# Attention and two feed-forward blocks on one core: splits spread over a border, norms and masks reordered, a small addition moved to GpSimd

## The chip, the cores and the metric

The kernel runs on 1 core of one Trainium2 chip. The metric is the device time of one execution in microseconds. In the profile PE is TensorE (matmul and transpose), PEld its weight loads, DVE VectorE, ACT ScalarE, POOL GpSimd, and SP the engine whose queue issues nearly all transfers. Every engine works through its own instructions strictly in their order and waits for the others by semaphores.

## The reference

```python
q_assign = argmax(q_n . c_n); k_assign = argmax(k_n . c_n)      # per head, 16 clusters
mask     = q_assign[:, :, :, None] == k_assign[:, :, None, :]
scores   = where(mask, scale * q @ k.T, -1e9)
attn     = exp(scores - max); attn = attn / (sum(attn) + 1e-9)
x        = (attn @ v), heads side by side                       # 1536 x 512
x        = ((x @ w1) * (x @ w2)) @ w3 @ w_out                   # 512 -> 1024 -> 1024 -> 512
h        = x @ w_in
out      = (max(h, 0) + alpha * min(h, 0)) @ moe2_w_out         # 512 -> 2048 -> 512
```

There are 2 batches, 8 heads, 768 positions and 64 numbers per head, all in float32.

## The kernel before

**Attention.** A head is a unit of 6 tiles of 128 queries, so there are 96 tiles; the loop at the end of the listing walks over them with index i. In step i the engines get, in this order: the transposes of tile i-4 (`emit_T`, L502), the scores of tile i+1 (`emit_S`, L462 for the products and L463 for the part that carries the cluster masks), for every second tile the sums' reciprocal (`emit_r`), the multiplication by it of tile i-2 (`emit_norm`, POOL, L488), the copies of the transposed tile out of PSUM (`emit_evac`, half on ACT L509, half on DVE L510), the row maximum of tile i+1 (`emit_max`, DVE, L470) and the exponential of tile i (`emit_exp`, ACT, L477); every second step ends with the products with v (`emit_PV`, L519). The scores have two PSUM buffers, the transposed tile one pair.

**Heads.** While a unit runs, the next head is prepared by `h_split` in pieces 0 to 5: piece 0 is three operations on POOL (L421, L422, L426), pieces 1 to 3 are copies by DMA, piece 4 sends the two cluster masks (L440, L441), piece 5 loads the head after it. A table by tile of the unit says which piece goes out when.

**Jobs.** `job(b, g)` works out the masks of four heads; its steps, and later the steps of the first layers, are spread over the attention steps by a generator (`fill`). The norms' square root stands in it (ACT L325) and needs another table on ACT than the exponential.

**Weights.** Each float32 weight tile is split into a high part and a low part (products are made of three fp32r matmuls). `w_step` does it in two halves: `w_conv` on DVE (L183, L184, L187; "a conversion" below), then the cast of the high part on ACT and the subtraction for the low part on POOL (L232). `w_goal` does one half, `w_pairs` loads tiles that were split before and kept in DRAM.

**The border.** The first layers of batch 0 (`l1`, tiles l1a and l1b, 12 matmuls each) run as fill work; l1a goes out through ACT, l1b through DVE (L580) which writes the product into PR. After them `x_split` splits the attention output of batch 1 (ACT L556; low parts on DVE and POOL, L558) into the buffer that batch 0's matmuls have just read, `p_split` splits the products PR of batch 0 (ACT L785, DVE L786: tile pl), and the first layers of batch 1 follow, with blocks of w3 (`lc`) between them. PR of batch 1 takes the same memory as PR of batch 0: as a new tile it can only be written when all splits of batch 0 are done. The PSUM tiles of this part are a ring of five, so TensorE may be at most five tiles ahead of what DVE and ACT have emptied.

Of the kernel before, what the change touches and what calls it, by code (L numbers as in the profile page):

```python
# [12 lines left out]
ALU = mybir.AluOpType  # L13
# [15 lines left out]
def kernel(  # L29
# [14 lines left out]
    nc = tc.nc  # L44
# [26 lines left out]
    seq, at, keep, need = [], {}, {}, {}  # L71
# [47 lines left out]
    NSEQ = len(seq)  # L119
# [116 lines left out]
    def w_goal(n):  # L236

        w_pairs(n)
        w_step(n)
# [213 lines left out]
    def emit_S(i):  # L453
        if i >= NU:
            return
        u, qt = unit(i)
        s = ST[u]
        t = pst("s", [P, 2, 512], f"s{i}", bufs=2)
        q = slice(qt * P, qt * P + P)
        for a in range(2):  # L460
            ks = slice(a * HS, a * HS + HS)
            nc.tensor.matmul(t[:, a, 0:HS], lhsT=s[:, 0, q], rhs=s[:, 1, ks], start=True, stop=False)  # L462
            nc.tensor.matmul(t[:, a, 0:HS], lhsT=s[0:80, 2, q], rhs=s[0:80, 3, ks], start=False, stop=True)  # L463
        scp[i] = t
# [16 lines left out]
        pt[i] = p  # L481

    def emit_r(g):
        nc.vector.tensor_scalar(out=sums[g], in0=sums[g], scalar1=1e-9, scalar2=None, op0=ALU.add)
        nc.vector.reciprocal(out=sums[g], in_=sums[g])  # L485

    def emit_norm(i):
# [61 lines left out]
    XS, PR = {}, {}  # L549
# [18 lines left out]

    def l1(b, f, a, alloc):

        if b not in PR:
            PR[b] = cp.tile([P, 8 * S], F32, tag="pr", name=f"pr{b}").rearrange("p (f s) -> p f s", f=8)
        t = alloc(f"l1a{b}{f}{a}")
        l1_mm(t[:, 0:HS], b, f, 0, a)
        q = wp.tile([P, HS], F32, tag="asb", name=f"asb{b}{f}{a}")
        nc.scalar.copy(out=q, in_=t[:, 0:HS])
        yield
        t = alloc(f"l1b{b}{f}{a}")
        l1_mm(t[:, 0:HS], b, f, 1, a)
        nc.vector.tensor_tensor(out=PR[b][:, f, a * HS : a * HS + HS], in0=t[:, 0:HS], in1=q, op=ALU.mult)  # L580
        yield


    with tc.manual_schedule():
# [46 lines left out]
        def l1_steps(b, f, ahead):  # L631
            for a in range(2):
                if a == 0:
                    w_ready(("l1", b, f, 1))
                for _ in l1(b, f, a, alloc_f):
                    w_goal(ahead)
                    yield f
# [10 lines left out]
        def fill_steps():  # L648

            yield from j01  # L650
            jm = cp.tile([P, 8 * S], F32, tag="wox", name="jm1")
            PR[0] = cp.tile([P, 8 * S], F32, tag="pr", name="pr0").rearrange("p (f s) -> p f s", f=8)
            sn = PR[0][:, 5:7].rearrange("p f s -> p (f s)")
            jmem[1, 0] = jm, jm[:, 3072 : 4608], jm[:, 5376 : 6144]
            jmem[1, 1] = jm, sn, PR[0][:, 7]
            for c in range(3):
                j_load(1, 0, c)
                yield
            j10, j11 = job(1, 0, alloc_f), job(1, 1, alloc_f)
            for k in range(5):  # L660
                next(j10)
                yield
            j_load(1, 1, 0)
            next(j10)
            yield
            for k in range(6):
                if k < 2:
                    j_load(1, 1, k + 1)
                next(j11)
                yield  # L670
            for _ in j10:
                yield
            for _ in j11:
                yield
            for _ in range(4):
                w_goal(at["l1", 0, 0, 1])
                yield
            while len(xdone) < 4:
                yield
            for f in range(8):  # L680
                yield from l1_steps(0, f, at["l1", 0, f, 0] + 3 if f < 6 else at["l1", 1, 0, 1])


        cur = [alloc_s]
# [10 lines left out]
            next(j00)  # L695
        next(j01)
        emit_S(0)
        emit_max(0)
        for _ in j00:
            pass  # L700
        cur[0] = alloc_r
        for k in range(2):
            next(j01)
        cur[0] = alloc_f
        nc.scalar.activation(out=warm, in_=warm, func=AF.Exp)
        nc.gpsimd.tensor_scalar(out=alp, in0=alp, scalar1=-1.0, scalar2=1.0, op0=ALU.mult, op1=ALU.mult)
# [7 lines left out]
        for i in range(NU + 8):  # L714
            if 0 <= i - LT < NU:
                emit_T(i - LT)
            if i + 1 < NU:
                emit_S(i + 1)

            if i >= 7 and i % 2 == 1 and (i - 7) // 2 < NU // 2:  # L720
                emit_x((i - 7) // 2)
            if i >= 2 and i % 2 == 0 and i // 2 - 1 < NU // 2:
                emit_r(i // 2 - 1)
            if 0 <= i - 2 < NU:
                emit_norm(i - 2)
            if 0 <= i - LT < NU:
                emit_evac(i - LT)
            if i + 1 < NU:
                emit_max(i + 1)
            if i < NU:  # L730
                emit_exp(i)
                u, j = unit(i)
                for k in ((0,), (1, 2), (3,), (4,), (5,), ())[j]:
                    h_split(u + 1, k)
            if i >= NU or i % 2 == 1 or i < 24 or 40 < i < 56:
                if fill_at[0] < (L1_B if i < NU else L1_D):
                    if next(fill) is not None:
                        fill_at[0] += 1
            if 10 <= i < 30 and i % 2 == 0:
                w_goal(at["l1", 0, 2, 0])  # L740
            if NUH + 4 <= i < NUH + 8:
                x_split(0, i - NUH - 4, 0)
                x_split(0, i - NUH - 4, 1)
                xdone.append(i)
            if i == NU - 1:
                late.append(i)
                for k in range(2):
                    w = st_tile(f"wo{k}").rearrange("p a n -> p (a n)").rearrange("p (g t n) -> p g t n", g=3, t=2)
                    for g in range(3):
                        WO[3 * k + g] = w[:, g, 0], w[:, g, 1]  # L750
            if i >= NU - 1:
                w_goal(at["wo", 0, 3, 0])

            k = i - 6
            if k >= 0 and k % 2 == 0 and k // 2 < NU // 2:
                emit_PV(k // 2)
                if k % 12 == 10:
                    v_load(k // 12 + 2)
# [31 lines left out]
        WO[6], WO[7] = (w[:, 0, 0], w[:, 0, 1]), (w[:, 1, 0], w[:, 1, 1])  # L790
        WO["wc"] = xp.tile([P, 2, 8, 512], F32R, tag="wc", name="wc")
        nsp = 0
        for f in fill:
            if f is not None and f < 7:
                w_goal(at["wo", 0, 5, 0])
            if f is not None and nsp < min(f, 6):
                p_split(0, nsp, 0), p_split(0, nsp, 1)
                nsp += 1
        for a in range(2):
            for p in range(4):  # L800
                x_split(1, p, a)
        while nsp < 8:
            p_split(0, nsp, 0), p_split(0, nsp, 1)
            nsp += 1
        for n, f in enumerate(BLOCKS):
            if f >= 0:
                for _ in l1_steps(1, f, NSEQ):
                    pass
            else:
                w_ready(("w3", 0, ~f, 1))  # L810
                lc(~f, alloc_c, lambda k: w_goal(NSEQ))
# [128 lines left out]
```

## Time and profile before

| what | us |
|---|---|
| median of 3 runs | 797.45 (797.44 to 798.0) |
| the profiled execution | 797.35 |
| its span, first to last instruction | 795.4 |
| TensorE busy in it | 758.0 |
| TensorE idle in it | 37.4 |

The kernel is bound by TensorE, so a time is read from the places at which TensorE is idle and from those at which its granted clock is halved. The attention lies from 22 to 314 us, the border from 314 to 370 us, and what follows is outside the change.

### The profile page before, as it was taken

To read this page: it belongs to the slowest core of one execution; us is meant where nothing else is said; L and a number is where in the kernel's file an instruction comes from. 1 tells how busy PE (TensorE), PEld (TensorE's weight loads), DVE (VectorE), ACT (ScalarE), POOL (GpSimd) and SP (SyncE) were. 2 spreads that over 40 slices of the span, in tenths; PEclk is the share of its full clock that TensorE was granted. 3 is DMA by queue.
4 is the path that set the end of the run, shared out by engine and by line. 5 is a ranking of instruction groups with operands and counts; after the bars stand their busy time and mean duration, and the time that the engine had idled before them with its cause. 6 is when DMAs were issued, how large, how long until landed. Compare 5 with 4: busy or idle time off the path is not lost.

```text
span 795.4 us, 13428 instructions
## 1 busy us (share of the span) xinstructions
PE 758.0 (95%) x5073; PEld 685.5 (86%) x5073; DVE 496.0 (62%) x833; ACT 393.5 (49%) x836; POOL 250.7 (32%) x228
## 2 busy tenths in 40 slices
PE   5789889989999999879999999999999999999998
PEld 2677778879999989879988999999998888899996
DVE  3778798995767777798455689324547763223222
ACT  5678766674555664364233345235444444333232
POOL 0466565684555633253222333001112220000000
PEclk9899999999999999989999999999999999999999
DMA  8657454253545517736444498016566637433332
GB/s 249 182 177 246 124 156 119 67 121 80 143 114 153 173 51 245 269 129 202 157 161 157 156 314 295 15 43 208 174 212 190 208 122 275 132 133 126 118 128 79
DMA packets 38863, 127.31 MB, mean 160 GB/s; under 512 B 5168, under 2 KB 5296, under 8 KB 38800
## 3 DMA queue, kind: packets, MB, share of 16 engines
q1 hardware_dynamic: 38800, 126.46, 50.8%
q8 instruction: 40, 0.66, 0.3%
q14 instruction: 23, 0.19, 0.1%
HBM read 84.08 MB, written 28.31 MB: 141 GB/s over the span
## 4 chain that ended last, share of the span: by engine, by line
PE 81%; DVE 5%; POOL 3%; issue 3%; ACT 3%; DMA 2%; SPq 1%; POOLq 0%; ACTq 0%; DVEq 0%
PE l L249 8%; PE l L251 8%; PE l L250 8%; PE t L502 7%; PE o L519 7%; PE acc L251 5%; PE acc L250 5%; PE acc L249 5%; PE s L463 4%; PE s L462 4%; PE l1a L250 3%; PE l1a L251 3%; PE l1a L249 3%; PE l1b L249 2%; PE l1b L251 2%
## 5 line engine op out<-in xcount | busy, mean ns | idle before, releaser
L232 POOL TENSOR_TENSOR wh<-wt,wh 128x512 fp32r<-128x512 f32 x64 | 86.7, 1355 | 241.3 <-ACT wh L231 120.7
L488 POOL TENSOR_SCALAR p<-p,su 128x768 f32<-128x768 f32 x96 | 88.6, 931 | 105.8 <-DVE su L485 44.1
L854 DVE SCALAR_TENSOR_TENSOR gr<-gr,alp 128x384 f32<-128x384 f32 x64 | 41.7, 651 | 109.1 <-ACT gr L853 109.1
L470 DVE TENSOR_REDUCE nm<-s 128x1 f32<-128x768 f32 x96 | 91.5, 953 | 10.4 <-PE s L463 8.6
L502 PE MATMUL t<-cst,p 128*128 128x128 f32 x576 | 85.0, 283 | 7.0 <-DVE pt L510 3.9
L477 ACT ACTIVATE p<-s,nm 128x768 f32<-128x768 f32 x96 | 87.0, 907 | 7.4 <-DVE nm L470 5.7
L502 PEld LDWEIGHTS t<-cst,p 128*128 128x128 f32 x576 | 66.5, 144 | 19.3 <-issue 7.3
L462 PE MATMUL s<-st 128*128 128x384 f32 x192 | 74.9, 390 | 3.6 <-ACT p L477 3.6
L251 PE MATMUL acc<-wh,g 128*128 128x512 f32 x192 | 75.3, 392 | 0.0
L249 PE MATMUL acc<-wh,g 128*128 128x512 f32 x192 | 74.8, 390 | 0.6 <-ACT os L878 0.6
L250 PE MATMUL acc<-wh,g 128*128 128x512 f32 x192 | 75.3, 392 | 0.0
L184 DVE SCALAR_TENSOR_TENSOR wt<-wr,wt 128x512 uint32<-128x512 uint32 x72 | 73.0, 1014 | 2.5
L519 PE MATMUL o<-pt,vs 128*64 128x128 f32 x1152 | 74.4, 279 | 0.0
L519 PEld LDWEIGHTS o<-pt,vs 128*64 128x64 f32 x1152 | 62.6, 138 | 12.5 <-issue 12.3
L852 ACT ACTIVATE gr<-l 128x384 f32<-128x384 f32 x64 | 31.2, 488 | 83.6 <-PE l L251 83.6
L463 PE MATMUL s<-st 80*128 80x384 f32 x192 | 67.0, 349 | 2.8 <-DMA st<-mk 2.8
L857 ACT CAST g<-gr 128x384 fp32r<-128x384 f32 x64 | 32.8, 513 | 58.7 <-DVE gr L854 58.7
L509 ACT COPY pt<-t 128x384 f32<-128x384 f32 x96 | 45.9, 478 | 31.6 <-PE t L502 30.9
L510 DVE COPY pt<-t 128x384 f32<-128x384 f32 x96 | 52.7, 549 | 12.3 <-PE t L502 11.3
L187 DVE SCALAR_TENSOR_TENSOR wt<-wu,wt 128x512 uint32<-128x512 uint32 x72 | 58.1, 808 | 2.5
L858 DVE TENSOR_TENSOR g<-gr,g 128x384 fp32r<-128x384 f32 x64 | 35.7, 558 | 37.1 <-ACT g L857 37.1
L231 ACT CAST wh<-wt 128x512 fp32r<-128x512 f32 x64 | 39.7, 620 | 32.8 <-DVE wt L187 13.8
(132 smaller groups left out, 1796.2 us busy)
## 6 DMA issues: line engine op xcount, KB each, us to landing
wh<-kept SPq DMA_DIRECT2D x58, 512.0 KB, 3.5
wr<-in_w_dram SPq DMA_DIRECT2D x48, 512.0 KB, 5.0
kept<-wh SPq DMA_DIRECT2D x48, 512.0 KB, 5.6
wr<-in_w3t_dram SPq DMA_DIRECT2D x16, 512.0 KB, 4.2
jm<-in_qka_dram SPq DMA_DIRECT2D x12, 512.0 KB, 5.3
hr<-in_qkh_dram SPq DMA_DIRECT2D x16, 384.0 KB, 3.5
st<-st SPq DMA_DIRECT2D x16, 384.0 KB, 3.7
st<-st SPq DMA_DIRECT2D x32, 192.0 KB, 2.7
```

The source lines that it names most:

```text
L184: nc.vector.scalar_tensor_tensor(out=t, in0=r[:, :, 0], scalar=29, in1=t, op0=ALU.logical_shift_right, op1=ALU.bitwise_or)
L232: nc.gpsimd.tensor_tensor(out=lo, in0=tts.pop(n), in1=f32(hi), op=ALU.subtract)
L249: nc.tensor.matmul(o, lhsT=whi, rhs=xhi, start=first, stop=False)
L250: nc.tensor.matmul(o, lhsT=whi, rhs=xlo, start=False, stop=False)
L251: nc.tensor.matmul(o, lhsT=wlo, rhs=xhi, start=False, stop=last)
L462: nc.tensor.matmul(t[:, a, 0:HS], lhsT=s[:, 0, q], rhs=s[:, 1, ks], start=True, stop=False)
L463: nc.tensor.matmul(t[:, a, 0:HS], lhsT=s[0:80, 2, q], rhs=s[0:80, 3, ks], start=False, stop=True)
L470: nc.vector.tensor_reduce(out=m, in_=scp[i][:, :, 0:HS], op=ALU.max, axis=AX.XY, negate=True)
L477: nc.scalar.activation(out=p.rearrange("p (a k) -> p a k", a=2), in_=scp.pop(i)[:, :, 0:HS], func=AF.Exp, bias=nmax.pop(i), scale=1.0, acc ...
L488: nc.gpsimd.tensor_scalar(out=pt[i], in0=pt[i], scalar1=sums[i // 2][:, i % 2 : i % 2 + 1], scalar2=1.0, op0=ALU.mult, op1=ALU.mult)
L502: nc.tensor.transpose(t[:, k], pt[i][:, kt * P : kt * P + P], ident)
L519: nc.tensor.matmul(ob[g][64 * j : 64 * j + 64], lhsT=v[:, u % 2, kt], rhs=pth[g][:, kt, j * P : j * P + P], start=(kt == 0), stop=(kt == N ...
```

## The change

There are five edits.

1. `emit_r` adds 1e-9 on POOL instead of DVE; the reciprocal stays on DVE.
2. The steps of `job(0, 1)` that make the norms of the second four heads are issued ahead of the first row maximum and of the first masks' writes.
3. Piece 4 of `h_split` (the masks) goes out with piece 3, one tile of the unit earlier than before; the other pieces keep their places.
4. Between i = 10 and 50 the weights' half steps are taken every fourth tile, where they were taken every second tile from 10 to 30. Conversions on DVE now stand at i = 12, 20, 28, 36 and 44, and stood at 10, 14, 18, 22 and 26.
5. PR of batch 1 is the same tile as PR of batch 0, so that its eighths are written as soon as the eighth's own split is done. Ahead of `x_split` two of the eight splits are made instead of six, the other six are spread over the first layers of batch 1. Two conversions move across in the same direction.

```diff
 def emit_r(g):
-    nc.vector.tensor_scalar(out=sums[g], in0=sums[g], scalar1=1e-9, scalar2=None, op0=ALU.add)
+    nc.gpsimd.tensor_scalar(out=sums[g], in0=sums[g], scalar1=1e-9, scalar2=1.0, op0=ALU.add, op1=ALU.mult)
     nc.vector.reciprocal(out=sums[g], in_=sums[g])
...
 def l1(b, f, a, alloc):
+    if b == 1:
+        PR[1] = PR[0]
...
-                yield from l1_steps(0, f, at["l1", 0, f, 0] + 3 if f < 6 else at["l1", 1, 0, 1])
+                yield from l1_steps(0, f, at["l1", 0, f, 0] + 3 if f < 6 else at["wo", 0, 3, 0] if f < 7 else at["l1", 0, 7, 1])
...
         emit_S(0)
+        cur[0] = alloc_r
+        for k in range(2):
+            next(j01)
         emit_max(0)
         for _ in j00:
             pass
-        cur[0] = alloc_r
-        for k in range(2):
-            next(j01)
...
-                for k in ((0,), (1, 2), (3,), (4,), (5,), ())[j]:
+                for k in ((0,), (1, 2), (3, 4), (), (5,), ())[j]:
                     h_split(u + 1, k)
...
-            if 10 <= i < 30 and i % 2 == 0:
+            if 10 <= i < 50 and i % 4 == 0:
                 w_goal(at["l1", 0, 2, 0])
...
-        for f in fill:
-            if f is not None and f < 7:
-                w_goal(at["wo", 0, 5, 0])
-            if f is not None and nsp < min(f, 6):
+        def more(n):
+            nonlocal nsp
+            if nsp < n:
                 p_split(0, nsp, 0), p_split(0, nsp, 1)
                 nsp += 1
+        for k, f in enumerate(fill):
+            w_pairs(at["l1", 1, 1, 1])
+            if f is not None and f < 7 and k % 2 == 0:
+                more(3)
         for a in range(2):
             for p in range(4):
                 x_split(1, p, a)
-        while nsp < 8:
-            p_split(0, nsp, 0), p_split(0, nsp, 1)
-            nsp += 1
         for n, f in enumerate(BLOCKS):
             if f >= 0:
-                for _ in l1_steps(1, f, NSEQ):
-                    pass
+                for k, _ in enumerate(l1_steps(1, f, NSEQ)):
+                    if f < 3:
+                        w_goal(NSEQ)
+                    if k % 2 == 0:
+                        more(8)
```

TensorE's own order does not change anywhere. The rows below show the other engines' orders at three places; the number behind a name tells buffers apart.

On DVE, behind `x_split`, before (pl is a low part of a split of batch 0, wt three operations of a conversion, pr the product of a pair of tiles of batch 1):

```order
L786 TENSOR_TENSOR pl_4071<-pr_488,ph_4070 128x384
L786 TENSOR_TENSOR pl_4075<-pr_488,ph_4074 128x384
L183 TENSOR_SCALAR wt_4281<-wu_4158 128x512
L184 SCALAR_TENSOR_TENSOR wt_4281<-wr_4092,wt_4281 128x512
L187 SCALAR_TENSOR_TENSOR wt_4281<-wu_4158,wt_4281 128x512
L580 TENSOR_TENSOR pr_4257<-l1b_4287,asb_4271 128x384
L183 TENSOR_SCALAR wt_4322<-wu_4285 128x512
L184 SCALAR_TENSOR_TENSOR wt_4322<-wr_4124,wt_4322 128x512
L187 SCALAR_TENSOR_TENSOR wt_4322<-wu_4285,wt_4322 128x512
L580 TENSOR_TENSOR pr_4257<-l1b_4328,asb_4316 128x384
```

The same engine and place now:

```order
L582 TENSOR_TENSOR pr_490<-l1b_4248,asb_4230 128x384
L183 TENSOR_SCALAR wt_4264<-wu_4240 128x512
L184 SCALAR_TENSOR_TENSOR wt_4264<-wr_4057,wt_4264 128x512
L187 SCALAR_TENSOR_TENSOR wt_4264<-wu_4240,wt_4264 128x512
L183 TENSOR_SCALAR wt_4291<-wu_4268 128x512
L184 SCALAR_TENSOR_TENSOR wt_4291<-wr_4107,wt_4291 128x512
L187 SCALAR_TENSOR_TENSOR wt_4291<-wu_4268,wt_4291 128x512
L788 TENSOR_TENSOR pl_4069<-pr_490,ph_4068 128x384
L788 TENSOR_TENSOR pl_4073<-pr_490,ph_4072 128x384
L582 TENSOR_TENSOR pr_490<-l1b_4303,asb_4285 128x384
```

Between two pr there was one conversion; now there are two and a split, four times in a row (the six pairs of tiles get C S pr, four times C C S pr, then S pr, with C a conversion and S a split; before they got S S, then six times C pr).

On POOL, at the border between units 5 and 6, before (hr and st are the pieces of the next head, p the attention rows, su their sums):

```order
L421 TENSOR_SCALAR hr_1282<-hr_1282,cst 128x768
L422 TENSOR_SCALAR st_1350<-hr_1282 128x768
L426 TENSOR_TENSOR st_1350<-hr_1282,st_1350 128x768
L488 TENSOR_SCALAR p_1322<-p_1322,su_1279 128x768
L488 TENSOR_SCALAR p_1348<-p_1348,su_1347 128x768
```

The same engine and place now:

```order
L421 TENSOR_SCALAR hr_1249<-hr_1249,cst 128x768
L422 TENSOR_SCALAR st_1323<-hr_1249 128x768
L426 TENSOR_TENSOR st_1323<-hr_1249,st_1323 128x768
L488 TENSOR_SCALAR p_1295<-p_1295,su_1246 128x768
L484 TENSOR_SCALAR su_1320<-su_1320 128x2
L488 TENSOR_SCALAR p_1321<-p_1321,su_1320 128x768
```

The addition L484, for which DVE's reciprocal waits, now stands behind the head's three operations and one multiplication.

On SP, at the masks of unit 2, before (jm is the load of 512 KB for the masks of batch 1, hr a head, mk the masks):

```order
L436 DMA st_412<-st_412 64x768
L265 DMA jm_487<-in_qka_dram 128x1024
L440 DMA st_412<-mk_210 16x768
L441 DMA st_412<-mk_210 16x768
L265 DMA jm_487<-in_qka_dram 128x1024
```

The same queue and place now:

```order
L436 DMA st_412<-st_412 64x768
L440 DMA st_412<-mk_210 16x768
L441 DMA st_412<-mk_210 16x768
L265 DMA jm_489<-in_qka_dram 128x1024 x2
L401 DMA hr_552<-in_qkh_dram 128x768
```

The masks go out directly behind the head's last copy, and the first load of jm behind them.

## Rows read from the trace of the kernel before

**Rows 1.** The page: busy time, share and instructions of TensorE.

```profile
PE 758.0 (95%) x5073; PEld 685.5 (86%) x5073; DVE 496.0 (62%) x833; ACT 393.5 (49%) x836; POOL 250.7 (32%) x228
```

**Rows 2.** Waits of PE: who <- for whom: us in total, times, longest.

```profile
PE l1a L249 <- ACT xs L556: 5.7, 1, 5.7
...
PE t L502 <- DVE pt L510: 3.9, 4, 1.7
PE s L462 <- ACT p L477: 3.6, 2, 2.9
...
PE s L463 <- DMA st<-mk: 2.8, 2, 2.1
PE t L502 <- POOL p L488: 2.1, 4, 1.1
```

**Rows 3.** Windows: start:end us, busy us by engine, PEclk, DMA share, GB/s.

```profile
53.00:57.00 4.00, 4.00 (x25) 3.10 (x28) 2.47 (x5) 1.55 (x4) 1.79 (x2) 0.57 0.89 352
...
94.00:98.00 4.00, 4.00 (x34) 3.67 (x29) 2.05 (x5) 2.21 (x6) 3.59 (x4) 0.57 0.00 0
...
340.00:346.70 6.70, 3.69 (x10) 3.29 (x11) 6.63 (x13) 6.34 (x16) 3.18 (x2) 0.50 0.15 62
```

**Rows 4.** Timeline at unit 2's masks: start, duration, instruction, [idle before].

```profile
47.71 0.54 SPq L265 DMA_DIRECT2D jm<-in_qka_dram  x1
...
48.30 0.56 SPq L440 DMA_DIRECT2D st<-mk  x1
...
52.12 1.06 ACT L278 ACTIVATE jm<-jm 128x1024 f32<-128x1024 f32 x1 [0.56 <-DMA jm<-in_qka_dram]
```

**Rows 5.** Timeline, TensorE behind the conversion of i = 22.

```profile
92.50 0.55 PE L502 MATMUL t<-cst,p 128*128 128x128 f32 x3 [1.75 <-DVE pt L510]
```

**Rows 6.** Timeline at i = 36 to 38, where a conversion is put in.

```profile
126.46 0.95 DVE L470 TENSOR_REDUCE nm<-s 128x1 f32<-128x768 f32 x1
...
127.81 0.56 DVE L510 COPY pt<-t 128x384 f32<-128x384 f32 x1
...
128.50 0.82 PE L502 MATMUL t<-cst,p 128*128 128x128 f32 x6
```

**Rows 7.** Timeline at the border of units 5 and 6, DVE and POOL.

```profile
114.93 1.83 POOL L426 TENSOR_TENSOR st<-hr,st 128x768 fp32r<-128x768 f32 x1
116.74 1.78 POOL L488 TENSOR_SCALAR p<-p,su 128x768 f32<-128x768 f32 x2
...
115.02 1.77 DVE L484 TENSOR_SCALAR su<-su 128x2 f32<-128x2 f32 x1
```

**Rows 8.** Timeline, TensorE in the first layers of batch 1.

```profile
341.84 0.69 PE L249 MATMUL l1a<-xs,wh 128*128 128x384 f32 x1 [5.74 <-ACT xs L556]
...
343.70 0.69 PE L250 MATMUL l1a<-xs,wh 128*128 128x384 f32 x1 [1.17 <-DVE xs L558]
...
357.50 0.33 PE L249 MATMUL l1a<-xs,wh 128*128 128x384 f32 x1
...
359.58 0.33 PE L249 MATMUL l1b<-xs,wh 128*128 128x384 f32 x1
```

**Rows 9.** Timeline of DVE and POOL about the border of the batches.

```profile
328.74 1.80 DVE L786 TENSOR_TENSOR pl<-pr,ph 128x384 fp32r<-128x384 f32 x2 [1.10 <-ACT ph L785]
...
343.52 6.27 POOL L558 TENSOR_TENSOR xs<-xr,xs 128x384 fp32r<-128x384 f32 x4 [4.03 <-ACT xs L556]
...
355.21 0.55 DVE L580 TENSOR_TENSOR pr<-l1b,asb 128x384 f32<-128x384 f32 x1
...
358.51 0.55 DVE L580 TENSOR_TENSOR pr<-l1b,asb 128x384 f32<-128x384 f32 x1
```

**Rows 10.** Timeline of DVE: two conversions in a row, later on.

```profile
412.20 0.42 DVE L183 TENSOR_SCALAR wt<-wu 128x512 uint32<-128x512 uint32 x1
...
413.99 0.42 DVE L183 TENSOR_SCALAR wt<-wu 128x512 uint32<-128x512 uint32 x1
...
415.17 1.66 DVE L187 SCALAR_TENSOR_TENSOR wt<-wu,wt 128x512 uint32<-128x512 uint32 x1
```

## The prediction, on record before the changed kernel ran

> **What bounds the kernel now.** The first thing to read is the page's line of busy times [rows 1]: TensorE works 758.0 of 795.4 us, every other engine far less. A change that takes no product away can gain only in the 37.4 us in which TensorE idles and in the stretches in which its clock is halved. So I read the waits of TensorE next [rows 2]: 5.7 us for the first high part of x (xs), 2.8 us for masks (st<-mk), 2.1 us for the multiplication on POOL (p), 3.6 us for exponentials. The windows [rows 3] add what such a wait leaves behind: behind the mask wait (53 to 57 us) and the wait at i = 22 (94 to 98) the granted clock is 0.57 on the mean, and from 340.0 to 346.7 it is 0.50, the lower level of 1.2 GHz, behind 5.74 us without work. The timelines [rows 4 to 10] then tell what each wait hangs on. The profiled execution took 797.35 us against a median of 797.45, so the sum is made on 797.35 and the 0.1 us is left out.
>
> **The change, part by part.** TensorE's order stays, so each part is a question of what TensorE waits for.
>
> *A. Norms ahead of the first maximum and masks.* Nothing is added. The first attention tile waits for its exponential (3.6 us over two waits, [rows 2]); norms issued earlier put some small DVE and ACT work ahead of the first maximum, but the square root then has left ACT before the first masks, and the next masks come sooner. I take -0.5 us, between -1.0 (a third of that wait) and +0.5.
>
> *B. Masks a tile earlier.* On SP the masks of unit 2 are issued at 48.30 us, behind a jm load issued at 47.71 [rows 4], and TensorE waits 2.10 of the 2.8 us [rows 2] for them at 52.76. Now they go first, so they are ahead of 512 KB in the queues. Removed: 2.10, the 0.7 of unit 5, and in 53 to 57 us 0.43 of 4.00 us of clock, so 1.7 [rows 3]: 4.5 in all. Against it: the jm load is issued some 1.2 us later (two issues of about 0.56 and their gaps), and ACT's square, which at 52.12 had already waited 0.56 us for it [rows 4], comes later by as much; products of the next masks stand behind it on TensorE in the same stretch. So most of the first wait is changed for another and the clock may fall all the same. I take -2.0, between -4.5 and +0.6 (the jm delay alone, half of 1.2).
>
> *C. Conversions spread over i = 12 to 44.* Five conversions are moved, none added up to there. At their old places TensorE waited four times for the copy of pt that stood behind one on DVE, 3.9 us in all [rows 2], 1.75 of it at i = 22 [rows 5], and behind that one the clock lost 0.43 of 4 us, 1.7 [rows 3]. Of the 1.75 I leave 0.8 to ACT's change of tables, so -4.8. At the new places from i = 28 on the step is at its tightest: from the maximum at 126.46 to the transposes at 128.50 are 2.04 us, of which the maximum and the copy (0.95 and 0.56) leave 0.5 [rows 6]. A conversion takes 1.79 us (412.20 to 413.99, [rows 10]), so it puts the copy behind it, and TensorE, about 1.3 us back; that for i = 28, 36 and 44 is +3.9. Net -0.9, between -4.8 (slack in the two PSUM buffers hides them) and +0.6 (a price of 1.8 each).
>
> *D. The addition on POOL.* At the border of units 5 and 6 POOL's last operation for the next head runs from 114.93 to 116.76, and DVE's addition to two numbers, started at 115.02, takes 1.77 us and ends with it [rows 7]. So DVE is blocked there whichever way the addition goes. Now the addition stands on POOL behind that operation and behind one multiplication as well, two of which take 1.78 us [rows 7]. DVE's reciprocal waits for it, and behind the reciprocal on DVE are queued the copy of pt and the next maximum, for which TensorE and then ACT wait. It is held by one multiplication (0.89) and two hand-overs longer than before, by my estimate 1.12 us. By the order on POOL this happens at the units' borders from i = 12 to 30, five times; at one of them two multiplications are ahead (2.09). Total 4 x 1.12 + 2.09 = 6.6 us, of which I charge 0.6, +4.0, because the copy of the odd tile has some of the 0.5 us of rest. Against it a few blocked additions away from the borders are gone and part of the 2.1 us of waits for POOL [rows 2], -0.5. So +3.5, between -0.5 and +6.6. After some 180 us TensorE is never late by so much that this shows.
>
> By the Trainium skill, "SBUF — State Buffer", section "Who interferes with whom", DVE and POOL share a port pair, and whoever issues first holds it for the whole instruction while the other is fully blocked; the trace agrees with the 1.77 us that end with POOL's operation. By the rule taken alone an addition off DVE frees DVE, and D would be -0.5 or better. The order on POOL speaks against that, so my sum doesn't use it.
>
> *E. The border.* This is the largest. Removed: TensorE stops 5.74 us for the first xs and 1.17 for its low part, and runs the tile between at half the clock [rows 8, 3], where it loses half of the 4.9 us that it works from 341.84 to 346.7, 2.45. Now four splits of batch 0 fewer lie ahead of `x_split`, so the casts of xs can follow the last matmul at 336.10 (341.84 - 5.74). That is up to -9.4 us at the first tile of batch 1.
>
> But the splits come back on DVE, between products. A tile of 12 matmuls takes 2.08 us (357.50 to 359.58, [rows 8]), a pair 4.16, and before one pair cost DVE 3.30 us (355.21 to 358.51, one conversion and pr, [rows 9]): DVE kept up. Now four pairs in a row need two conversions, a split and pr. A conversion alone takes 1.79 us and one directly behind another 2.84 (413.99 to 416.83, [rows 10]), since POOL's subtraction for the first blocks it; a split's low parts end 2.90 us after the conversion (1.10 waiting for ACT's ph, then 1.80, [rows 9]); pr 0.55, overlapping by some 0.1. That is about 7.9 us a pair against 4.16. TensorE may be five tiles ahead, no more, so it is held back by 3.7 us for each pair once the ring is full. The chain: TensorE could begin at about 336.7; POOL's four xs subtractions take 6.27 us [rows 9], to 343.1, and slow the conversions of the first pair; its split and pr end at 346.8. The first w3 block needs the tile of the fourth pair: 346.8 + 3 x 7.9 = 370.5. Before, it began at 341.84 + 1.17 + 2.45 + 12 x 2.08 = 370.4. So the 9.4 us are given back in whole; and the block's second half (2.8 us later before) now needs a conversion that stands behind the splits, about 1.0 to 1.5 us late. I take +1.5, between -7 (DVE keeps pace, the POOL subtractions still cost 2) and +4 (a halved clock through the waits).
>
> Sum: -0.5 - 2.0 - 0.9 + 3.5 + 1.5 = **+1.6 us**, so 797.35 + 1.6 = 799.0, with the 0.1 us to the median 799.1.
>
> **The rivals.**
>
> *R1, DVE keeps pace at the border (faster).* The cycle of 7.9 us is built from contended durations. Bare, it is 2 x 1.79 + 1.0 + 0.5 = 5.0. TensorE's own work would then end at 336.7 + 12 x 2.08 = 361.7, and the chain gives 346.8 + 3 x 5.0 = 361.8, 8.6 us before 370.4; the late conversion of the block costs 1.5 of it, so E is about -7 and the time 799.1 - 1.5 - 7 = 790.6. It decides from a cycle of 7.4 us down (1.5 / 3 less than 7.9), from which on E is a gain. For it: the blocked part varies in the rows. Against it: each conversion is followed by its POOL subtraction.
>
> *R2, the holds and late conversions are hidden (faster).* If the tiles' double buffers take the 1.1 us of D and the 1.3 of C, D is -0.5 and C -4.8: 799.1 - 4.0 - 3.9 = 791.2. For it: TensorE idles only 2.1 us for POOL now. Against it: a single conversion stopped TensorE for 1.75 us [rows 5].
>
> *R3, holds and conversions cost in full (slower).* One mechanism: an in-order DVE is stopped behind a POOL operation or a conversion, and TensorE by the whole of it: D +6.6, C +0.6, E +4: 799.1 + 3.1 + 1.5 + 2.5 = 806. It decides as soon as D and E together exceed by 1.6 us the 3.4 that A, B and C bring.
>
> *R4, the change does not do what it says.* The masks wait for the producer anyway, and xs waits for ACT's queue, not for the splits: B and E about 0, C and D together +2.6 or less: 797.5 to 800.
>
> **How the numbers follow.** Forecast 0.37 (797 to 802), R1 0.20 (790.6), R2 0.15 (791), R3 0.14 (806), R4 0.14. A difference of 0.2%, 1.6 us, is about what a measurement of this kernel can tell from none: 795.85 to 799.05. Faster: R1, R2 and 0.01 of the forecast, 0.36. Same: 0.17 of the forecast and half of R4, 0.24. Slower: 0.19, R3 and the other half, 0.40. The predicted time is 799.1; the range takes in R1 and R2 and the lower part of R3, 790.5 to 805.5; the likeliest case's own is 797 to 802.
>
> **What would show it.** A: the first exponential wait of TensorE under 2.9 us. B: no wait for st<-mk near 52 us; if instead one for ja of about 1 us stands there with the clock at half, the exchange is right. C: none of the four old waits for pt, and three waits for pt of about 1.3 behind i = 28, 36 and 44. D: reciprocals with an idle of 1 us or so before them, put down to POOL's su, at five borders. E: the first l1a of batch 1 by 337 with waits under 1 us, then TensorE waiting for pr about 3.7 us a pair from the third pair on, and w3's first block beginning near 370.5. It is wrong if these waits do not come: then the cycle of DVE is under 6 us, or the holds fall into TensorE's own slack, and the time is nearer to 791.

## The result: 1.45% slower, and the profile after

The changed kernel takes 809.0 us (median of 4, 807.88 to 809.68) against 797.45 us before: a ratio of 1.0145, with a 95% interval of 1.0127 to 1.0162, 11.6 us more. The forecast was 799.1, the range 790.5 to 805.5: it forecast a small loss and the loss is seven times as large. The profiled execution of the changed kernel has a span of 807.8 us, 12.4 more than the 795.4 of before. From the page of the changed kernel, the engines' busy times:

```profile
PE 764.2 (95%) x5073; PEld 687.9 (85%) x5073; DVE 481.7 (60%) x785; ACT 393.7 (49%) x836; POOL 262.2 (32%) x276
```

TensorE's 5073 instructions are the same ones in the same order, but they are busy for 764.2 us instead of 758.0 [rows 1]: 6.2 of the 12.4 us are waits, and 6.2 lie in instructions that take longer, a part of it at the lower clock shown below. What TensorE waits for in the changed kernel (us in total, times, longest):

```profile
PE t L502 <- DVE pt L510: 10.5, 11, 2.8
...
PE ja L288 <- ACT jm L278: 4.1, 4, 2.0
PE l1a L249 <- DVE pr L582: 3.5, 2, 2.8
PE lc L249 <- DVE pr L582: 2.9, 1, 2.9
PE t L502 <- POOL p L488: 2.8, 3, 1.4
PE jc L332 <- DVE mk L389: 1.9, 1, 1.9
...
PE s L462 <- ACT p L477: 0.8, 2, 0.6
...
PE l1a L249 <- ACT xs L556: 0.6, 1, 0.6
```

Set against [rows 2], everything that the change aims at came true: no wait for masks is left, the exponentials' 3.6 us are 0.8, the 5.7 us for xs are 0.6. But the wait for the copy pt has gone from 3.9 us (4 times) to 10.5 (11 times), and two waits for pr of 2.8 and 2.9 us and one of 1.9 for mk are new.

Since TensorE's order is the same, the lag of the changed kernel can be read off at any instruction that stands in both traces. The first products of batch 0's l1a behind the attention, in the trace of before and then of after:

```profile
319.16 0.45 PE L249 MATMUL l1a<-xs,wh 128*128 128x384 f32 x1 [0.72 <-DVE pr L580]
```

```profile
329.41 0.44 PE L249 MATMUL l1a<-xs,wh 128*128 128x384 f32 x1 [0.72 <-DVE pr L582]
```

The lag is 10.25 us ahead of the border. At the end of the border it is 12.0. So the border, the largest item of the forecast, costs some 2 us, as forecast, and the attention, for which the sum had A to D at +0.1, costs 10. Followed through the attention in the same way the lag is -2.2 us at 54 us, +2.1 at 67, -2.4 at 107, +3.0 at 135, +7.1 at 170 and +10.1 at 190 us of the changed kernel's time. Both sides are one execution each, and small lags can't be put down to an edit: at 54 us border_only and border_swap below, in which nothing is changed up to there, have -2.6 and -0.9. The lag rises at few places, and the granted clock is at its lower level (0.50, 1.2 GHz) behind four of them, at 64, 132, 187 and 381 us. Three of these (windows of the changed kernel: start:end, busy us by engine, PEclk, DMA share, GB/s):

```profile
64.00:67.00 3.00, 3.00 (x32) 2.19 (x26) 0.53 (x1) 0.75 (x3) 1.03 (x2) 0.50 0.80 251
186.70:190.10 3.40, 3.40 (x12) 3.40 (x12) 1.72 (x4) 0.93 (x2) 2.15 (x4) 0.51 0.46 138
381.30:384.70 3.40, 3.40 (x9) 2.67 (x9) 3.33 (x5) 2.63 (x6) 1.43 (x1) 0.50 0.69 236
```

The first rise is at i = 12 (timelines of ACT, DVE and TensorE in the changed kernel):

```profile
52.84 1.06 ACT L278 ACTIVATE jm<-jm 128x1024 f32<-128x1024 f32 x1 [0.98 <-DMA jm<-in_qka_dram]
...
56.46 1.26 ACT L178 ACTIVATE wu<-wr 128x512 f32<-128x512 f32 x2
...
57.20 2.06 DVE L183 TENSOR_SCALAR wt<-wu 128x512 uint32<-128x512 uint32 x1 [3.28 <-ACT wu L178]
...
62.27 0.55 PE L502 MATMUL t<-cst,p 128*128 128x128 f32 x3 [2.81 <-DVE pt L510]
```

The conversion of i = 12 needs a copy wu that ACT makes. ACT has it in its order behind two squares of jm, and the first square waits 0.98 us for the load that edit 3 sends later. DVE stands 3.28 us in front of the conversion, then works slowly beside POOL (2.06 us for an operation of 0.42), and TensorE waits 2.81 us and runs at half clock. In conv_only below, without edit 3, it still waits 2.33 us here.

A later rise, at the start of unit 8 (units counted from 0), i = 50 (POOL, then DVE, of the changed kernel):

```profile
163.25 1.83 POOL L426 TENSOR_TENSOR st<-hr,st 128x768 fp32r<-128x768 f32 x1
165.03 1.26 POOL L232 TENSOR_TENSOR wh<-wt,wh 128x512 fp32r<-128x512 f32 x1
166.28 0.91 POOL L488 TENSOR_SCALAR p<-p,su 128x768 f32<-128x768 f32 x1
167.27 0.19 POOL L484 TENSOR_SCALAR su<-su 128x2 f32<-128x2 f32 x1
...
167.50 0.17 DVE L485 RECIPROCAL su<-su 128x2 f32<-128x2 f32 x1 [3.48 <-POOL su L484]
```

DVE stands for 3.48 us with the copy of pt queued behind the reciprocal. A weight's subtraction (L232, the second half of a conversion, from i = 48) stands in POOL's row there as well. In all the reciprocal waits for POOL twelve times:

```profile
DVE su L485 <- POOL su L484: 17.4, 12, 3.5
```

### The profile page after: what moved, and what is told of

It is laid out like the page before. It is cut to its first block, busy times and chain, and to the rows that moved or that the text cites. A ratio compares the mean times of both kernels' runs of the same rounds, so it can differ in the third digit from the quotient of the medians.

```text
span 807.8 us, 13409 instructions
## 1 busy us (share of the span) xinstructions
PE 764.2 (95%) x5073; PEld 687.9 (85%) x5073; DVE 481.7 (60%) x785; ACT 393.7 (49%) x836; POOL 262.2 (32%) x276
## 4 chain that ended last, share of the span: by engine, by line
PE 76%; DVE 8%; POOL 5%; ACT 4%; issue 3%; DMA 3%; SPq 1%; POOLq 0%; DVEq 0%; ACTq 0%
PE l L251 8%; PE l L249 8%; PE l L250 7%; PE o L519 6%; PE t L502 6%; PE acc L251 5%; PE acc L250 5%; PE acc L249 5%; PE s L462 3%; PE s L463 3%; PE l1a L250 2%; PE l1a L249 2%; PE l1a L251 2%; PE l1b L249 2%; PE l1b L251 2%
## 5 line engine op out<-in xcount | busy, mean ns | idle before, releaser
L232 POOL TENSOR_TENSOR wh<-wt,wh 128x512 fp32r<-128x512 f32 x64 | 86.7, 1355 | 241.5 <-ACT wh L231 127.9
L502 PE MATMUL t<-cst,p 128*128 128x128 f32 x576 | 86.1, 283 | 14.4 <-DVE pt L510 10.5
L184 DVE SCALAR_TENSOR_TENSOR wt<-wr,wt 128x512 uint32<-128x512 uint32 x72 | 69.6, 966 | 2.5
L187 DVE SCALAR_TENSOR_TENSOR wt<-wu,wt 128x512 uint32<-128x512 uint32 x72 | 61.7, 858 | 2.5
```

Source lines behind the costliest of these rows:

```text
L184: nc.vector.scalar_tensor_tensor(out=t, in0=r[:, :, 0], scalar=29, in1=t, op0=ALU.logical_shift_right, op1=ALU.bitwise_or)
L232: nc.gpsimd.tensor_tensor(out=lo, in0=tts.pop(n), in1=f32(hi), op=ALU.subtract)
L502: nc.tensor.transpose(t[:, k], pt[i][:, kt * P : kt * P + P], ident)
```

## The experiments

Ratios are against the kernel before, run beside them on the same chip; the intervals are of 95%.

**One edit at a time.** Four kernels hold one edit of the diff each; their edits are edits 5, 1, 4 and 3 of the diff shown, word for word.

border_only (edit 5):

> Only edit 5 is made. Theory: at the border the cast of xs comes some 9 us earlier, and TensorE gives it all back waiting for pr, with a stretch at half clock: +1.5 to +2 us, about 799. First rival (DVE keeps pace when nothing else is changed): -7 us, about 790.5. Second rival (the border is what makes the changed kernel slow): +6 us or more.

Measured: 1.0018 (1.0006 to 1.003), about +1.4 us. The theory holds. The rows of DVE's products, of one of its splits, and of TensorE's first block of w3 in this kernel:

```profile
345.25 0.55 DVE L582 TENSOR_TENSOR pr<-l1b,asb 128x384 f32<-128x384 f32 x1
...
351.44 1.81 DVE L788 TENSOR_TENSOR pl<-pr,ph 128x384 fp32r<-128x384 f32 x2 [1.10 <-ACT ph L787]
353.18 0.54 DVE L582 TENSOR_TENSOR pr<-l1b,asb 128x384 f32<-128x384 f32 x1
...
361.15 0.55 DVE L582 TENSOR_TENSOR pr<-l1b,asb 128x384 f32<-128x384 f32 x1
...
369.12 0.55 DVE L582 TENSOR_TENSOR pr<-l1b,asb 128x384 f32<-128x384 f32 x1
...
369.81 0.47 PE L249 MATMUL lc<-wo,wh 128*128 128x512 f32 x1 [0.80 <-DVE pr L582]
```

The cycle is 7.93, 7.97 and 7.97 us (forecast 7.9) and the block begins at 369.81 (forecast 370.5). This stretch also runs at half clock from 361 to 368 us, behind a wait of 2.78 us.

add_only (edit 1):

> Only edit 1 is made. Theory: the addition on POOL holds DVE's reciprocal behind whatever POOL has queued, also beyond 150 us where a weight subtraction or an x subtraction stands there too: +5 to +7 us, about 803.5. First rival (the holds cost only where a conversion has used up the rest as well): within 1.5 us of before. Second rival (the addition off DVE frees DVE): -1 to -3 us.

Measured: 1.0071 (1.0045 to 1.0098), about +5.7 us. Both rivals fall.

conv_only (edit 4):

> Only edit 4 is made. Theory: the four old waits and their half clock are gone (-4.8), but the conversion of i = 12 now waits on ACT behind the squares of the next norms and stops TensorE by some 3 us and a half clock (+4.5), and i = 20, 28 and 36 by 1 to 2 each (+4): about +4, 801. Rival (the step of the prediction, -0.9): 796.5. Second rival (two buffers hide them): 793.

Measured: 1.0085 (1.0066 to 1.0103), about +6.8 us: the theory's sign, and more than it said. The step of the prediction (-0.9) falls by far.

masks_only (edit 3):

> Only edit 3 is made. Theory: the waits of 2.10 and 0.7 us for masks and the half clock behind the first are gone, a wait of 1 us for ja takes the place of a part: about -3 us, 794.5. Rival (the later jm load gives all back): within 1 us of before.

Measured: 0.9989 (0.9977 to 1.0001), about -0.9 us. In the trace the waits for masks are gone, but over whole runs the gain is a third of what the theory said, and the interval takes in no gain; the rival stands.

The four add up to 1.4 + 5.7 + 6.8 - 0.9 = 13.0 us against 11.6 measured together. To see whether the rest of the change (with the norms, which were not run alone) has a part in the loss, edits 1 and 4 were taken out of the changed kernel:

> Edits 2, 3 and 5 alone: the changed kernel with the addition back on DVE and the conversions back at i = 10 to 26. Theory (edits 1 and 4 make the loss, and the rest adds up from the single runs, +1.4 for the border and -0.9 for the masks, with the norms about +0.4): within 1.5 us of before, 797 to 799. Rival (the norms, or edits that only hurt together, have a part in it): +4 us or more.

Measured: 0.998 (0.9968 to 0.9992), -1.6 us. Without edits 1 and 4 the change is a small gain. The whole loss is the addition on POOL and the conversions' new places. The border and the masks alone were +1.4 and -0.9, so the difference that is left for the norms is about -2.1 us, known to some 1.7.

**The addition.** add_ahead issues the addition directly behind its exponential:

```diff
     def emit_r(g):
-        nc.vector.tensor_scalar(out=sums[g], in0=sums[g], scalar1=1e-9, scalar2=None, op0=ALU.add)
         nc.vector.reciprocal(out=sums[g], in_=sums[g])
...
                 emit_exp(i)
+                if i % 2 == 1:
+                    nc.gpsimd.tensor_scalar(out=sums[i // 2], in0=sums[i // 2], scalar1=1e-9, scalar2=1.0, op0=ALU.add, op1=ALU.mult)
```

> The kernel before, with the addition on POOL but issued directly behind the exponential that it needs, ahead of the next head's three operations, of the weight subtraction and of the x subtraction. Theory (the cost of edit 1 is where the addition stands in POOL's order): nearly all of the +5.7 us of add_only is gone, within 1.5 us of before, 797 to 799; no wait of the reciprocal above 1 us. Rival (a hand-over from POOL to DVE on every second tile costs by itself, or POOL is too full): +4 us or more still.

Measured: 1.0031 (1.0015 to 1.0047), about +2.5 us, more than the 1.5 that the theory allowed and less than the rival's 4. The expectation was wrong in one point: at the units' borders nothing moved, because the addition needs the exponential of a unit's second tile, and the head's operations are issued at the first. Only the places past them moved, and the reciprocal's holds still come to 16.3 us in all, against 17.8 in add_only. Both kernels at i = 56, where x is split: of each DVE and TensorE, and then a window behind the stop, add_only first:

```profile
180.61 0.17 DVE L485 RECIPROCAL su<-su 128x2 f32<-128x2 f32 x1 [3.01 <-POOL su L484]
...
181.28 0.90 PE L502 MATMUL t<-cst,p 128*128 128x128 f32 x3 [1.34 <-DVE pt L510]
```

```profile
182.00:185.50 3.50, 3.50 (x12) 3.50 (x12) 1.97 (x5) 0.99 (x2) 1.65 (x3) 0.50 0.54 146
```

```profile
176.90 0.17 DVE L484 RECIPROCAL su<-su 128x2 f32<-128x2 f32 x1 [2.05 <-POOL su L732]
...
177.58 0.55 PE L501 MATMUL t<-cst,p 128*128 128x128 f32 x3 [0.38 <-DVE pt L509]
```

```profile
177.60:181.00 3.40, 3.40 (x21) 3.37 (x22) 2.57 (x5) 1.12 (x4) 2.90 (x5) 1.00 0.60 126
```

One x subtraction (0.99 us) ahead of the addition or behind it makes a hold of 3.01 or 2.05 us, a stop of 1.34 or 0.38, and 6.8 us at half clock or none: some 4 us from this one place in these two executions. The traced one of add_only (805.22 us) is the slowest of its five, whose median is 803.29, and by the medians the two kernels are 3.2 us apart. In the changed kernel the same place has a stop of 1.35 us and half clock for 3.4 us.

no_add leaves the addition out (`emit_r` keeps only its second line):

> The kernel before without the addition of 1e-9 (left out; the reciprocal is taken of the sums as they are). It prices what taking the addition off DVE can bring at most. Theory (the reciprocal is then blocked by POOL in its place): within 1 us of before. Rival (by the port rule alone the blocked 8 us of the additions come free): -3 to -6 us.

Measured: 0.9995 (0.998 to 1.001), no difference. So there was next to nothing to be had from DVE's addition in the first place: at most 0.2%, by the interval. The time is the theory's, but not for its reason, since the reciprocal isn't blocked in the addition's place. This one runs while POOL's last operation for the next head (L426) lasts from 115.95 to 117.78 us:

```profile
117.48 0.16 DVE L484 RECIPROCAL su<-su 128x2 f32<-128x2 f32 x1
```

What blocked the addition is plain, 1.77 us that end with POOL's operation [rows 7]. By the Trainium skill, "SBUF — State Buffer", section "Who interferes with whom", DVE and POOL contend for a shared port pair, which one of them gets for a whole instruction while the other is blocked; the trace agrees for the addition. A DVE that is free at these places is still worth no more than the runs show.

late_head and add_free try to get rid of the last 2.5 us by issuing the head's operations one tile later (late_head), with add_ahead's addition before them (add_free):

```diff
-                for k in ((0,), (1, 2), (3,), (4,), (5,), ())[j]:
+                for k in ((), (0,), (1, 2), (3, 4), (5,), ())[j]:
```

> The kernel before with the next head's three POOL operations, its copies and third copy each one tile later (the masks stay). A control for add_free: the addition stays on DVE. Theory: DVE's addition is no longer caught by the last of the three operations, but the multiplications behind them are later: within 2 us of before.

> As late_head, with the addition on POOL directly behind its exponential, so ahead of the next head's three operations. Theory (the cost of edit 1 is only where the addition stands on POOL): no wait of DVE's reciprocal above 0.6 us at the units' borders, and the time within 1 us of late_head. Rival (each hand-over from POOL to DVE costs by itself): 2 us or more above late_head.

Measured: late_head 1.0049 (1.0034 to 1.0063), +3.9 us, add_free 1.0215 (1.019 to 1.0239), +17 us. Both expectations failed. In late_head TensorE waits 1.71 us for a copy of the next head (st) at 110.06 us and runs at half clock for 6.8 us about it; its lag to the kernel before rises there by 3.7 us, nearly its whole loss. In add_free the addition was where it should be, and the holds of the reciprocal went down from the 17.8 us of add_only to 8.0 in all (the longest 1.9, where 0.6 was expected), but what POOL now does later is waited for. In add_free, a row of POOL, and then of TensorE's waits:

```profile
111.72 0.91 POOL L487 TENSOR_SCALAR p<-p,su 128x768 f32<-128x768 f32 x1 [2.83 <-DVE su L484]
```

```profile
PE t L501 <- POOL p L487: 4.8, 6, 1.1
...
PE s L463 <- DMA st<-mk: 3.9, 8, 0.6
PE s L462 <- DMA st<-st: 3.7, 5, 0.9
```

POOL stands 2.83 us for a reciprocal of DVE, with the head's operations behind it, and TensorE waits eight times for a head's masks and five times for its copies. Such waits of POOL aren't new, though: for the reciprocal it stands 44.1 us in all here and 47.6 in late_head. New is that it also waits 64.2 us, at 32 places, for the exponential ahead of the addition. Why add_free is 13 us slower than late_head isn't shown further than that. The rival's number came true; the addition has another place in POOL's order as well as another engine, so what a hand-over between POOL and DVE costs by itself stays open.

**The conversions.** conv_phase2 and conv_third shift and tighten the raster, conv_early keeps all conversions ahead of i = 28, conv_moved takes edit 4's raster and moves only the four half steps that fall on a unit's first tile. All four change this one line of the kernel before.

conv_phase2:

```diff
-            if 10 <= i < 30 and i % 2 == 0:
+            if 10 <= i < 50 and i % 4 == 2:
```

> The kernel before with the half steps at every fourth tile from 10 to 46, so conversions at i = 10, 18, 26, 34 and 42 in place of 12, 20, 28, 36 and 44. The first one's copies on ACT then stand ahead of the squares. Theory: the stop at 60 to 67 us of conv_only (2.3 us and a half clock) is gone, the tight tiles at 34 and 42 cost as much as 28, 36 and 44 did: about +2 to +3 us, 800. Rival (the first one's place is no matter, the loss is in the tight tiles alone): +6 us, 803.5.

Measured: 1.0077 (1.0054 to 1.0101), +6.2 us. The stop at 62 us is gone, as the theory said, yet the loss is that of conv_only, the rival's number: the conversion of i = 42, a unit's first tile, lasts 3.9 us, and TensorE waits 3.1 us behind it at 146 us for a step of the masks' job (pr, L347), with 6.8 us at half clock; the lag rises by 4.7 us there.

conv_third:

```diff
-            if 10 <= i < 30 and i % 2 == 0:
+            if 10 <= i < 40 and i % 3 == 1:
```

> The kernel before with the half steps at every third tile from 10 to 37, so conversions at i = 10, 16, 22, 28 and 34, none at a unit's first tile, where POOL prepares the next head; two of them are behind i = 28. First theory (from i = 28 on DVE has no rest, 96% busy without any conversion against 65% from 8 to 28, so each conversion there costs what it lasts): 2 x 2.4 in, 2 out, so +2 to +4 us, 800. Second theory (it is the meeting with POOL's operations at a unit's first tile that makes a conversion dear): within 1 us of before or below.

Measured: 0.999 (0.9977 to 1.0004), no difference. The conversions of i = 28 and 34 last 2.5 and 2.3 us and stop TensorE for 1.39 and 0.68 us, about the 1.3 that the prediction took; the gains at the old places pay for that.

conv_early:

```diff
-            if 10 <= i < 30 and i % 2 == 0:
+            if i in (10, 12, 14, 15, 16, 17, 20, 21, 26, 27):
```

> The kernel before with conversions at i = 10, 14, 16, 20 and 26, their second halves at 12, 15, 17, 21 and 27: all ahead of i = 28, none at a unit's first tile. Both theories on the conversions: the waits at i = 18 (1.05) and 22 (1.75, half clock) lose the part that a conversion makes: -1 to -3 us, 795.5. Rival (a wait is only moved to where the conversion now stands): within 1 us of before.

Measured: 1.0016 (1.0003 to 1.003). The rival is nearer: the waits are only moved (1.67 us at 73.66, 1.62 at 106.67, and one of 1.99 for ACT's copy at 80.90).

conv_moved:

```diff
-            if 10 <= i < 30 and i % 2 == 0:
+            if i in (14, 16, 20, 25, 28, 32, 38, 40, 44, 49):
```

> conv_only with the half steps of i = 12, 24, 36 and 48 moved to 14, 25, 38 and 49: conversions at 14, 20, 28, 38 and 44, none of the ten half steps on a unit's first tile, three conversions still behind i = 28. Theory (the meeting with POOL's operations is what makes them dear): about 1.3 us for each conversion behind i = 28 and 5 us of old waits gone, so -1 to +1.5 us, 797 to 799. Rival (the spread into the full stretch is what costs): +5 us or more, 802.5, as in conv_only.

Measured: 1.0068 (1.0046 to 1.009), +5.4 us. The theory falls: without any half step on a unit's first tile edit 4 costs nearly the same. The conversions do become short (2.5 us at i = 38, where the one at i = 36 took 4.3), but in this trace TensorE waits at 137.04 us for something else (SP's queue and TensorE):

```profile
129.51 0.46 SPq L436 DMA_DIRECT2D st<-st  x1
130.06 0.54 SPq L138 DMA_DIRECT2D wr<-in_w_dram  x1
130.69 0.40 SPq L149 DMA_DIRECT2D kept<-wh  x1
131.14 0.57 SPq L440 DMA_DIRECT2D st<-mk  x1
...
137.04 0.41 PE L463 MATMUL s<-st 80*128 80x384 f32 x1 [2.49 <-DMA st<-mk]
```

The half step of i = 38 issues a weight's load and a store on SP, and both now stand between the head's last copy and the masks, which go out 1.1 us later for it. That they also take longer from there to TensorE (from the second one's issue to the product 5.2 us, no more than 2.5 in the kernel before) isn't explained by the rows. In conv_only a wait of 1.00 us for masks at 157.64 stands behind the conversion of i = 44 in the same way.

**Other orders, and a faster kernel.** border_swap is edit 5 with two lines exchanged:

```diff
                 for k, _ in enumerate(l1_steps(1, f, NSEQ)):
+                    if k % 2 == 0:
+                        more(8)
                     if f < 3:
                         w_goal(NSEQ)
-                    if k % 2 == 0:
-                        more(8)
```

> Only edit 5 is made, but each split of batch 0 stands ahead of the added half step, so between DVE's conversion and POOL's subtraction of it and not behind both. Theory (the cycle of 7.9 us at the border is made of the 1.10 us hand-over and of blocked low parts): the cycle comes down to about 6.1 us, the first block of w3 begins 5 us earlier: -3 to -5 us, 793.5. Rival (the amount of conversions, not their order, sets the cycle; or the block waits for its own weights): as border_only, 798 to 799.

Measured: 0.9951 (0.9934 to 0.9968), -3.9 us. The same conversions, splits and products, and the sign is turned. DVE in this kernel, and the first block of w3:

```profile
345.11 0.55 DVE L582 TENSOR_TENSOR pr<-l1b,asb 128x384 f32<-128x384 f32 x1
...
350.13 1.01 DVE L788 TENSOR_TENSOR pl<-pr,ph 128x384 fp32r<-128x384 f32 x2
351.07 0.55 DVE L582 TENSOR_TENSOR pr<-l1b,asb 128x384 f32<-128x384 f32 x1
...
357.67 0.55 DVE L582 TENSOR_TENSOR pr<-l1b,asb 128x384 f32<-128x384 f32 x1
...
364.95 0.47 PE L249 MATMUL lc<-wo,wh 128*128 128x512 f32 x1 [0.87 <-DVE pr L582]
```

The low parts take 1.01 us with no wait ahead of them, where they took 1.81 behind a wait of 1.10: ACT makes the high parts while DVE still converts, and POOL's subtraction comes behind them. The cycle is 5.96 and 6.60 us instead of 7.97, and the block begins 4.9 us earlier.

masks_swap adds edit 3 to it, and masks_swap_third the raster of conv_third:

> Edit 3 and edit 5 with each split ahead of the added half step; additions, conversions and norms as before. Theory (the gains of the two are in different stretches and add up, -0.9 and -3.9): 792 to 793, below both kernels. Rival (a faster attention only lets the border wait longer): 794 or more.

> masks_swap with the half steps at every third tile as in conv_third. Theory (a conversion is dear where it meets POOL's operations at a unit's first tile; with none there the four old waits are gone and two of 1.4 and 0.7 us come): 1 us below masks_swap, 791, and no conversion above 2.6 us up to 130 us. Rival (no difference, as conv_third alone against before): 792.

Measured: masks_swap 792.05 us, 0.9932 (0.9913 to 0.995); masks_swap_third 791.49 us, 0.993 (0.9907 to 0.9953). Both beat both kernels. The last step isn't told apart from no difference.

## Why the prediction was wrong, point by point

**A, the norms.** Not run alone. The trace shows the exchange: the exponential's 2.90 us are gone, TensorE waits 1.95 us for mk instead, and the clock is at half from 26.3 us instead of from 29.3; at 31 us the lag is +0.2. About nothing in this trace, where -0.5 was taken; the difference of the runs above leaves about -2.1, known to some 1.7. The size isn't settled.

**B, the masks.** The mechanism is as told (the wait for masks goes, 1.04 us for ja comes). The size was taken at -2.0 and is -0.9 in masks_only, within its bounds. It was read from one trace, and the wait differs between executions: in the ten others that send these masks as before it is 1.31 to 2.46 us, and the lower clock follows it in four of them.

**C, the conversions: the step that failed.** -0.9 was taken, between -4.8 and +0.6, and edit 4 alone costs 6.8: that is 7.7 of the 9.9 us by which the forecast fell short. What it removes was taken too large. Of the four waits for pt, 3.9 us in all, only the two at 79.86 and 92.50 us (1.05 and 1.75) stand behind a conversion; ahead of the others DVE has a maximum of the masks' job (L341) and a split of x (L558). And the lower clock behind i = 22, 1.7 us, belongs to that one execution: eleven other traces have the same wait of 1.74 or 1.75 us, with the clock at its upper level behind it in all. With the 0.8 us left to ACT that makes -2.0, not -4.8, and by the step's own price of +3.9 a loss of 1.9. (In conv_only the lag to the trace of before falls by some 5 us between 67 and 106 us, these 1.7 among them.)

What it adds was priced at three conversions of 1.3 us from i = 28 on. Three things were left out. The conversion of i = 12 was given no price, though ACT's copies for it now stand behind the squares of jm (3.7 us of lag in conv_only between 61 and 67 us, with half clock in the end of it; conv_phase2, where they stand ahead, doesn't have it). The price of a bare conversion, 1.79 us, was used where POOL works beside it: at i = 36 it lasts 4.3 us, as these rows of the changed kernel show (DVE, then POOL),

```profile
127.11 0.86 DVE L183 TENSOR_SCALAR wt<-wu 128x512 uint32<-128x512 uint32 x1
...
129.23 2.20 DVE L187 SCALAR_TENSOR_TENSOR wt<-wu,wt 128x512 uint32<-128x512 uint32 x1
...
128.75 2.14 POOL L426 TENSOR_TENSOR st<-hr,st 128x768 fp32r<-128x768 f32 x1
```

and in the changed kernel half clock (132 to 135.5 us) comes behind it, which wasn't priced; conv_only has none there. And a half step was taken as work of DVE alone, though it issues a load and a store on SP, which in conv_moved and conv_only stand ahead of the masks. The stretch in which these fall has little rest to take them. Two windows of the trace of before:

```profile
60.00:105.00 45.00, 41.59 (x419) 34.09 (x417) 37.05 (x71) 35.17 (x71) 26.23 (x25) 0.96 0.62 180
105.00:158.00 53.00, 50.36 (x501) 44.48 (x500) 48.06 (x91) 36.22 (x84) 32.77 (x33) 1.00 0.43 113
```

From 105 to 158 us DVE, the third of the busy times, works for 48.06 of 53 us with no conversion at all (91%; the 96% in an expectation above added instructions that overlap). From 60 to 105 it works for 37.05 of 45 us, four conversions of 1.8 to 4.5 us among them. The rest of 0.5 us that the step read at one pair of rows [rows 6] was the slack of one tile in a stretch that has 0.2 a tile on the mean (4.9 us over its 22 tiles). How the loss behind i = 28 divides among these isn't settled: conv_third has two conversions there and loses some 3 us between 104 and 166 us, conv_moved has three and loses some 10, of which the rows show 2.1 behind the first with half clock for 3.4 us, and 2.5 and 1.1 for masks.

**D, the addition.** +3.5 was taken, the upper bound 6.6, and it costs 5.7: the mechanism was right, the size too small. The step counted five borders, up to i = 30. In add_only the reciprocal has holds of 0.54, 2.87 and 2.63 us at three of these and none to speak of at a fourth (81 us), and seven more of 0.97 to 3.01 us behind them, which the sum didn't hold. The largest piece in the trace lies at 181 us (some 177 in the time of the kernel before), where an x subtraction is in the same row on POOL and half clock for 6.8 us follows the stop. That POOL's order speaks against the port rule's gain held.

**E, the border.** +1.5 was taken and +1.4 measured, with the cycle at 7.9 against 7.97 us. This part is right by its own steps, but for the form of the waits: instead of 3.7 us a pair from the third pair on, border_only has waits of 2.78 and 0.80 us for pr and a stretch at half clock between them. Half clock (361 to 368 us in border_only), which stood only in the upper bound, is a part of the price.

**The rivals.** R1 (DVE keeps pace, 790.6) was named for the right reason: the cycle decides. The changed kernel doesn't do it; border_swap, at 6.0 to 6.6 us, does, below the 7.4 at which it was said to turn. R2 and R4 are out. R3 is the nearest: holds and conversions cost in full. It gave C no more than +0.6, and so ended at 806.

## What to carry to other kernels

When an in-order engine's work is moved, price each new place, not the work: what stands ahead of it on every engine that feeds it, what runs beside it there, which transfers it issues and what those stand ahead of. Look at the share of busy time over the whole stretch that must take it, not at the slack of one tile. Don't price a wait, or the clock behind it, from one execution: here the same wait had half clock behind it in one trace and not in eleven others. And where two engines hand work back and forth, try the exchange of two lines before giving up the idea: the same border work was +1.4 us in one order and -3.9 in the other.

## What the runs showed of the hardware

A stop of TensorE of 1.34 us at 181 us was followed by 6.8 us at the lower clock, one of 0.38 at the same work was not (the rows of add_only and add_ahead above); this stop was therefore worth 3.4 us more than its length. The length of a stop alone doesn't settle it: 1.75 us at i = 22 had the lower clock behind it in the trace of before [rows 3, 5], and 1.74 or 1.75 us at the same place had the upper level behind it in eleven other traces. DVE's reciprocal of 128x2 takes 0.15 to 0.17 us beside POOL's operations (eleven times in no_add), where the addition on the same two columns took up to 1.77 [rows 7]: of two operations of the same size one is caught and the other isn't.
